# Projection units in groups of four, half of them opened by the lower rows, and fewer GpSimd splits in layer 1

## The chip, the cores and the metric

One core of a Trainium2 chip. The metric is the time of one execution of the whole kernel in microseconds of the device. Engines are named as in the profile: PE is TensorE (PEld its weight loads), DVE is VectorE, ACT is ScalarE, POOL is GpSimd, SP is SyncE, whose queue issues nearly all DMAs.

## The reference

Two layers, each attention and then a dense part, with the same weights in both layers. Everything is fp32; S = 2048 rows, D = 640, H = 32 heads of Dh = 20, F = 1536.

```python
def _A_ref(x, wqkv, wo):
    qkv = transpose((x @ wqkv).reshape(B, S, 3, H, Dh), 2, 0, 3, 1, 4)
    q, k, v = qkv[0], qkv[1], qkv[2]
    scores = einsum("bhqd,bhkd->bhqk", q, k) * (Dh ** -0.5)
    p = softmax(scores)
    o = einsum("bhqk,bhkd->bhqd", p, v)
    return transpose(o, 0, 2, 1, 3).reshape(B, S, D) @ wo

def _B_ref(x, w1, b1, w2, b2):
    h = relu(einsum("bsd,df->bsf", x, w1) + b1) ** 2
    return einsum("bsf,fd->bsd", h, w2) + b2

for _ in range(2):
    x = x + _A_ref(layernorm(x), wqkv, wo)
    x = x + _B_ref(layernorm(x), w1, b1, w2, b2)
```

## The kernel before

**Precision.** Every fp32 matrix is split into a high part in the matmul's own rounded format and a low part, the rest. A product of two matrices is three matmuls: high by high, high by low, low by high. A split is made in one of two ways: `split_to` (L253; ACT casts the high part out of the bank at L255, DVE subtracts at L256) or `split_on_pool` (L258; ACT copies the bank to SBUF at L262, POOL casts at L267 and subtracts at L270).

**Stages of a layer.** The projections (`qkv`, L674), attention (L932), then the output projection and the dense part. In attention each of 512 key tiles takes a score matmul (L556), an exponential on ACT (L563) and two matmuls with v (L568).

**The projections.** There are 72 units of work. 40 of them give a group of 128 columns of q or k for a block of 512 rows (`tb` is the block, `pos` the column group; the first sixteen are pos 0 to 3 of the blocks 0 to 3). 32 give half of the columns of v for 128 rows (`tt`, `hf`). A unit is 2 x 15 products into one PSUM bank. 15 contract over the upper 64 rows of the array and 15 over the lower 64 rows, and the two halves of the array can work at the same time on different units (`product`, L302; all products have line L320). Both halves add to the same bank. Where the upper 15 are done, a tiny copy on ACT (L322), the mark, is tied to the last of them, and the first lower product waits for the mark. The open units' banks are a ring of four (`ps_pj`).

`work_on` gives one stream of rows its next product; the upper stream and the lower stream both go through the units in order, and the lower one starts when the upper one is a unit and nine products (`LAG`) ahead. When the lower one ends a unit, `end` evicts it: q and k by `end_qk` (a split, three-fold stores to DRAM, L76 on SP; of the first k units also differences, kd), v by `end_v` (a copy on ACT, L368). Loads of q, k and kd from DRAM come back as operands of score matmuls.

**What is put between the products.** `front` (L376) prepares the normalised, transposed and split input of a block (x scaled at L251, transposes at L393 or, for block 0 of layer 1, L1259, splits of five pieces `xnT`), a step at a time. `insert` puts score matmuls (L474) for the row maxima of softmax between the products. Such a score takes either the upper or the lower half of the rows, and they come in pairs. A maximum is then taken by DVE (L486), or by ACT (L495) and DVE together (L503). A planner with estimated times of the engines (`now`, `busy`) chooses which score goes in and when; all this is settled while the program is built. What maxima are not placed in the projections are placed in attention, where cycles of eight key tiles take 12 or more pairs of them.

**The main loop** of the projections runs over j, 72 + 2 units, and offers each stream an insertion, else a product:

```python
while at_now[0] < (j + 1) * N and at_now[1] < len(chains) * N:
    if not insert(0):
        work_on(0)
    if not insert(1) and at_now[0] - at_now[1] > N + LAG + (not at_now[1]):
        work_on(1)
```

In layer 1 the weights of the first four column groups are cast and split first (`begin_first`, L1243): two of them ahead of the loop and two in it, one of the latter with DVE's subtraction. Blocks 2 and 3 are split by POOL in both layers (`tb > 1`), blocks 0 and 1 by ACT and DVE.

Of the kernel before, what the change touches and what calls it, by code (L numbers as in the profile page):

```python
# [8 lines left out]
F32 = mybir.dt.float32  # L9
# [7 lines left out]
P = 128  # L17
# [5 lines left out]
KD = D // P  # L23
NF = F // P
QB = 512
# [14 lines left out]
def tile_layers(  # L40
# [26 lines left out]
    def slot(shape, dtype, label):  # L67
        return arena.tile(shape, dtype, tag="slot", name=name(label))
# [225 lines left out]
    def after(later, earlier):  # L294
        tc.add_manual_dep(
            later.ins,
            earlier.ins.name,
            mybir.DependencyInfo(mybir.DependencyClass.Sync, mybir.DependencyReason.DATA),
            reason="lower rows add to the bank that the upper rows have left",
        )  # L300

    def product(ch, n, r):  # L302

        what, a, b = ch["of"]
        rows = slice(64 * r, 64 * r + 64)
        k, t = divmod(n, 3)
        if what == "qk":
            hw, hx = THREE[t]
            w = w_qk.piece(b * 10 + hw * KD + k)[rows]
            x = xt_[a][k][rows, hx, :]  # L310
            pair, width = (w, x), QB
        else:
            tb, i = divmod(a, 4)
            hx, hw = THREE[t]
            x = xt_[tb][k][rows, hx, i * P : (i + 1) * P]
            pair, width = (x, w_v.piece(k * 4 + hw * 2 + b)[rows]), HALF
        first, last = r == 0 and n == 0, r == 1 and n == 3 * KD - 1
        if first:
            ch["dst"] = ps_pj("pj")
        m = nc.tensor.matmul(ch["dst"][:, :width], *pair, start=first, stop=last)  # L320
        if n == 3 * KD - 1 and r == 0:
            mark = nc.scalar.copy(mark_t[:, 0:1], mark_t[:, 1:2])  # L322
            after(mark, m)
            ch["upper"] = mark
        if n == 0 and r == 1:
            after(m, ch.pop("upper"))

    def end_qk(pos, tb, dst):
        ev = slot([P, 2, QB], F32R, "ev")
        which, jj = divmod(ORDER[pos], 5)  # L330
        rows = slice(jj * P, (jj + 1) * P)
        kd = None
        if which and pos < FIRST:


            if tb % 2 == 0 and jj == 0:
                keys["of"] = slot([P, 2, QB], F32, "kf")
            kf = keys["of"][:, jj, :]
            r = xtile("r")[:, :QB] if tb % 2 else kf
            if tb:  # L340
                split_on_pool(ev[:, 0, :], ev[:, 1, :], dst, r)
            else:
                split_to(ev[:, 0, :], ev[:, 1, :], dst)
                nc.scalar.copy(r, dst)
            if tb % 2:
                kd = slot([P, 2, QB], F32R, "kd")
                nc.gpsimd.tensor_sub(kf, r, kf)
                pool_hi(kd[:, 0, :], kf)
                pool_lo(kd[:, 1, :], kf, kd[:, 0, :].bitcast(F32))
                if jj:  # L350
                    del keys["of"]
        else:
            (split_on_pool if tb or pos > 3 else split_to)(ev[:, 0, :], ev[:, 1, :], dst)

        def store():
            thrice(d_qk[which, tb, rows], ev, 1 + which)
            if kd is not None:
                thrice(d_kd[tb // 2, rows], kd, 2)

        return store  # L360
# [12 lines left out]
            v = vs.pop(tt)  # L373
            return lambda: dma(nc.sync, d_v[tt * P : (tt + 1) * P], v)

    def front(tb, x_src, bank, each=1):  # L376

        rows = [row_tile(x_src, tb * 4 + i) for i in range(4)]
        yield 0, False
        mvs = []  # L380
        for x in rows:
            mvs.append(stats(x))
            yield 1.1, False
        for n, (x, mv) in enumerate(zip(rows, mvs)):
            normalise(nc.vector, x, mv)
            yield 0.65, n == 3
        res = []
        for k0 in range(0, KD, each):
            ks = range(k0, min(k0 + each, KD))
            dsts = [bank("xt") for _ in ks]  # L390
            for k, dst in zip(ks, dsts):
                for i in range(4):
                    nc.tensor.transpose(  # L393
                        dst[:, i * P : (i + 1) * P], rows[i][:, k * P : (k + 1) * P], ident
                    )
            for dst in dsts:
                t = slot([P, 2, QB], F32R, "xnT")
                (split_on_pool if tb > 1 else split_to)(t[:, 0, :], t[:, 1, :], dst)
                res.append(t)
            if len(res) == KD:  # L400
                xt_[tb] = res
                rows.clear()
            yield 0, len(res) < KD
# [270 lines left out]
    def qkv(first, x_src, rest):  # L674
# [11 lines left out]
        def at(when, n, f):  # L686
            when.setdefault(n, []).append(f)

        for pos in range(2 if first else FIRST, 10):
            n = UNITS.index((0, pos)) - 4 if pos >= FIRST else pos - 2  # L690
            if first:
                if pos >= FIRST:
                    at(early, n - 2, lambda pos=pos: raws.append(raw_cols(wqkv, ORDER[pos])))
                at(late, n, lambda pos=pos: w_qk.put(
                    raws.pop(0), pos * 10, pos * 10 + KD, KD, nc.scalar.copy,
                    nc.vector.tensor_sub if pos == 2 else pool_lo,
                ))
            else:
                at(early, n, lambda pos=pos: w_qk.need(pos * 10, pos * 10 + 9))
# [55 lines left out]
        def later(keep=0):  # L755
            while len(pending) > keep:
                pending.pop(0)()
# [79 lines left out]
        N, LAG = 3 * KD, 9  # L837

        def end(n):

            what, a, b = chains[n]["of"]
            dst = chains[n].pop("dst")
            now["act"] = max(now["act"], now["pe"]) + 0.6
            if what == "qk":
                pending.append(end_qk(b, a, dst))
                if b >= FIRST and a == NQB - 1 or n == 4 * FIRST - 1:
                    w_qk.past(b * 10 + 9, w_qk.got)
                return
            f = end_v(a, b, dst)
            if not b:  # L850
                return
            later()
            pending.append(f)
            if a % 4 == 3:
                del xt_[a // 4]
            if a == 14:
                for c in (1, 3):
                    if (2, c) not in k_t:
                        load_k(2, c, True)
            if a == 10:  # L860
                load_v(0, 0)
            if a == 12:
                for c in range(4):
                    assert (0, c) not in k_t
                    load_k(0, c, True)
                load_q(1)

        at_now = [0, 0]

        def work_on(r):  # L870
            n, m = divmod(at_now[r], N)
            at_now[r] += 1
            if n < len(chains):
                product(chains[n], m, r)
                if r and m == N - 1:
                    end(n)

        for j in range(len(chains) + 2):
            if j < len(UNITS):
                while UNITS[j][0] not in xt_:  # L880
                    step_rest()
                run(early, j)
            while at_now[0] < (j + 1) * N and at_now[1] < len(chains) * N:
                if not insert(0):
                    work_on(0)
                if not insert(1) and at_now[0] - at_now[1] > N + LAG + (not at_now[1]):
                    work_on(1)
                now["pe"] += 0.235 if j < len(UNITS) else 0.155
                state["n"] += 1
                if state["n"] % 4 == 0 and not state["turn"]:  # L890
                    step_rest()
# [2 lines left out]
                w_v.save_full(1)  # L894
            if j < len(UNITS):
                run(late, j)
                later(1)
            n = j - 2
            if 1 < n < NQB * FIRST + 2:
                b, step = divmod(n - 2, 4)  # L900
# [425 lines left out]
```

## Time and profile before

| | us |
|---|---|
| median of 3 runs | 3692.89 (3692.02 to 3696.78) |
| the profiled execution's own time | 3689.96 |
| its span in the profile | 3688.1 |
| mean granted TensorE clock | 0.993 |
| projections of layer 1 | 0 to 357 |
| attention, output and dense part of layer 1 | 357 to 1860 |
| projections of layer 2 | 1883 to 2178, with a start from 1860 |
| attention, output and dense part of layer 2 | 2178 to 3690 |

The stage bounds are where the first score of attention (L556) and the first products of a layer stand in the trace. A row of the profile's windows has, for each engine, busy us and the count of its instructions. A row of the groups has line, engine, operation, output and inputs, count, then busy us and mean ns of one, then idle us just before and what ended it. A row of the chain has start, length and what it was.

### The profile page before, as it was taken

How to read it: one execution, taken by the hardware profiler on the slowest of the kernel's cores; microseconds unless marked ns; L12 is line 12 of the kernel's file. 1: busy time of each engine (PE TensorE's matmuls, PEld its weight loads, DVE VectorE, ACT ScalarE, POOL GpSimd, SP SyncE). 2: the span in 40 equal slices, each digit the busy share in tenths (PEclk: the TensorE clock that was granted, in tenths of full speed). 3: DMA queues.
4: the chain of work that ended last, by engine and by line, in shares of the span. 5: the costliest groups of instructions: out<-in, count | busy, mean ns of one | idle time of the engine just before them, and what ended most of it. 6: DMA issues, size and time to landing. Idle time of an engine off the chain costs nothing.

```text
span 3688.1 us, 67591 instructions
## 1 busy us (share of the span) xinstructions
PE 3635.3 (99%) x25738; PEld 2174.8 (59%) x25738; DVE 2714.6 (74%) x5034; ACT 2655.9 (72%) x5217; POOL 823.6 (22%) x914
## 2 busy tenths in 40 slices
PE   7899999999999999999999999999999999999999
PEld 5788433434334335988888873343433434378998
DVE  6677999999999993344567779999999999723443
ACT  2577999999999996122226789999999999941221
POOL 6440334321122111111144202112112211201110
PEclk8999999999999999999999999999999999999999
DMA  7776554432222135611167753232232121373111
GB/s 231 240 271 184 148 164 135 138 82 65 60 54 58 36 91 175 248 43 43 58 214 268 236 153 81 66 77 60 67 79 55 47 57 45 109 248 139 43 48 38
DMA packets 256880, 429.45 MB, mean 116 GB/s; under 512 B 60624, under 2 KB 107472, under 8 KB 256556
## 3 DMA queue, kind: packets, MB, share of 16 engines
q1 hardware_dynamic: 255724, 422.77, 37.3%
q8 instruction: 202, 3.31, 0.4%
q10 hardware_dynamic: 832, 2.37, 0.2%
q14 instruction: 122, 1.00, 0.1%
HBM read 265.15 MB, written 159.88 MB: 115 GB/s over the span
## 4 chain that ended last, share of the span: by engine, by line
PE 94%; DMA 2%; DVE 2%; ACT 1%; POOL 1%; issue 0%; SPq 0%; ACTq 0%; DVEq 0%
PE banks L568 28%; PE banks L285 20%; PE banks L556 20%; PE banks L474 15%; PE banks L320 9%; DMA q<-d_qk 1%; POOL xnT L270 1%; DVE h L256 0%; DMA d_qk<-ev 0%; PE banks L1112 0%; DVE r L1139 0%; ACT h L255 0%; DMA raw<-in_A_wqkv_dram 0%; DMA k<-d_qk 0%; ACT r L1138 0%; PE banks L393 0%
## 5 line engine op out<-in xcount | busy, mean ns | idle before, releaser
L563 ACT ACTIVATE e<-banks 128x512 f32<-128x512 f32 x4096 | 2113.3, 604 | 61.3 <-PE banks L474 2.2
L486 DVE TENSOR_REDUCE mx<-banks 128x1 f32<-128x512 f32 x3040 | 1908.8, 684 | 222.0 <-PE banks L474 146.8
L474 PE MATMUL banks<-k,q 60*128 60x512 f32 x3568 | 1243.4, 428 | 22.3 <-DMA q<-d_qk 20.6
L556 PE MATMUL banks<-q,k 62*128 62x512 f32 x4096 | 1153.0, 436 | 0.9 <-ACT rl L495 0.9
L568 PE MATMUL banks<-e,vg 128*32 128x512 f32 x8192 | 1094.1, 606 | 0.0
L556 PEld LDWEIGHTS banks<-q,k 62*128 62x128 f32 x4096 | 600.3, 185 | 702.5 <-ACT e L563 670.9
L474 PEld LDWEIGHTS banks<-k,q 60*128 60x128 f32 x3568 | 582.1, 185 | 300.0 <-DVE mx L486 206.5
L503 DVE CUSTOM_DVE_ANT_0 rl<-banks,rl 128x512 f32<-128x512 f32 x528 | 345.5, 689 | 106.4 <-PE banks L474 90.8
L320 PE MATMUL banks<-xnT,wqk 64*128 64x512 f32 x2400 | 393.0, 400 | 3.1 <-DVE xnT L256 3.1
L568 PEld LDWEIGHTS banks<-e,vg 128*32 128x32 f32 x8192 | 162.1, 108 | 358.0 <-issue 331.7
L285 PE MATMUL banks<-w,h 128*128 128x320 f32 x2304 | 358.5, 313 | 5.9 <-DVE h L256 3.8
L495 ACT ACTIVATE rl<-banks 128x512 f32<-128x512 f32 x534 | 288.2, 600 | 99.7 <-PE banks L474 94.6
L285 PEld LDWEIGHTS banks<-w,h 128*128 128x128 f32 x2304 | 340.6, 189 | 15.4 <-DVE h L256 8.2
L285 PE MATMUL banks<-xnT,w 128*128 128x512 f32 x1440 | 330.0, 390 | 0.0
L320 PEld LDWEIGHTS banks<-xnT,wqk 64*128 64x128 f32 x2400 | 301.8, 190 | 37.6 <-DVE xnT L256 3.5
L1138 ACT ACTIVATE r<-banks,b_t 128x512 f32<-128x512 f32 x96 | 66.1, 689 | 356.7 <-PE banks L285 352.8
L285 PEld LDWEIGHTS banks<-xnT,w 128*128 128x128 f32 x1440 | 269.6, 188 | 55.0
L267 POOL CAST mr<-nt 128x32 fp32r<-128x32 f32 x64 | 13.4, 209 | 1197.5 <-DVE nt L529 1197.5
L612 POOL TENSOR_TENSOR few<-few,minus_t 128x16 f32<-128x16 f32 x62 | 179.8, 2900 | 152.6 <-DMA few<-d_s 152.6
L320 PE MATMUL banks<-wv,xnT 64*128 64x320 f32 x1920 | 200.5, 307 | 0.4 <-DMA wv<-d_wv 0.4
L1158 DVE TENSOR_TENSOR x<-banks,x 128x320 f32<-128x320 f32 x128 | 62.9, 492 | 182.9 <-PE banks L285 181.2
L320 PEld LDWEIGHTS banks<-wv,xnT 64*128 64x128 f32 x1920 | 190.9, 186 | 2.1 <-DMA wv<-d_wv 0.8
(78 smaller groups left out, 1969.3 us busy)
## 6 DMA issues: line engine op xcount, KB each, us to landing
q<-d_qk SPq DMA_DIRECT2D x256, 240.0 KB
d_qk<-ev SPq DMA_DIRECT2D x80, 512.0 KB
k<-d_qk SPq DMA_DIRECT2D x156, 240.0 KB
x<-d_x SPq DMA_DIRECT2D x88, 320.0 KB
d_qk<-ev SPq DMA_DIRECT2D x80, 256.0 KB
d_o<-ot SPq DMA_DIRECT2D x248, 80.0 KB
ot<-d_o SPq DMA_DIRECT2D x38, 512.0 KB
d_v<-v SPq DMA_DIRECT2D x32, 512.0 KB
```

What stands on the lines that cost most here:

```text
L285: nc.tensor.matmul(dst, a, b, start=(n == 0), stop=(n == last))
L320: m = nc.tensor.matmul(ch["dst"][:, :width], *pair, start=first, stop=last)
L474: nc.tensor.matmul(dst, q_t[t][b : b + 60, p, sub * P : (sub + 1) * P], k_t[t // NQB, c][b : b + 60, p, :], start=True, stop=True,)
L486: nc.vector.tensor_reduce(maxima(t)[:, 2 * par + p, sub, c : c + 1], dst, axis=AX.X, op=ALU.max)
L495: nc.scalar.activation(res, dst, AF.Relu)
L503: nc.vector.tensor_tensor_reduce(out=r, in0=dst, in1=r, scale=1.0, scalar=LEAST, op0=ALU.add, op1=ALU.max, accum_out=maxima(t)[:, 2 * par ...
L556: nc.tensor.matmul(dst, k_t[t // NQB, kt // 4][b : b + 62, p, (kt % 4) * P : (kt % 4 + 1) * P], q_t[t][b : b + 62, p, :], start=True, stop ...
L563: nc.scalar.activation(es[p][:, par, :], dst, AF.Exp, scale=SCALE)
L568: nc.tensor.matmul(acc[32 * h : 32 * h + 32, :], v_t[t // NQB, kt // 8][:, kt % 8, 32 * h : 32 * h + 32], es[p][:, par, :], start=(kt == 0 ...
L612: nc.gpsimd.tensor_tensor(few, few, minus_t, op=ALU.pow)
L1138: nc.scalar.activation(r, dst, AF.Relu, bias=b1_t[:, f : f + 1])
L1158: nc.vector.tensor_add(x[:, c], dst[:, :HALF], x[:, c])
```

## The change

Units are worked in groups of four. In each group the upper stream goes through units 0, 1, 2, 3 and the lower stream through 2, 3, 0, 1. So each stream opens two units and closes two, both streams start together and end together, and `LAG` goes. The mark works both ways: it stands between the half that opens a unit and the half that closes it. Two units are ended in the third and two in the fourth quarter of a group.

Since both streams use a group's units from the start, the order of the weights is changed: pos 0 and 2 ahead of the loop, pos 1 and 3 before its first unit, all of them with POOL's subtraction. `keys` counts its four users rather than being opened and dropped by block, the stores follow the order in which units end, and v's loads move accordingly.

Which `xnT` pieces POOL splits is now said by the caller of `front`: in layer 1, k = 1 of block 2 and k = 1 and 3 of block 3 (all five of each before). In layer 2, all of block 2 as before, and k = 1 and 3 of block 3 (all five before). The others go to `split_to`.

```diff
-    def product(ch, n, r):
+    def product(ch, n, r, opens):
...
-        first, last = r == 0 and n == 0, r == 1 and n == 3 * KD - 1
+        first, last = opens and n == 0, not opens and n == 3 * KD - 1
...
-        if n == 3 * KD - 1 and r == 0:
+        if n == 3 * KD - 1 and opens:
             mark = nc.scalar.copy(mark_t[:, 0:1], mark_t[:, 1:2])
             after(mark, m)
-            ch["upper"] = mark
-        if n == 0 and r == 1:
-            after(m, ch.pop("upper"))
+            ch["half"] = mark
+        if n == 0 and not opens:
+            after(m, ch.pop("half"))
...
-            for dst in dsts:
+            for k, dst in zip(ks, dsts):
                 t = slot([P, 2, QB], F32R, "xnT")
-                (split_on_pool if tb > 1 else split_to)(t[:, 0, :], t[:, 1, :], dst)
+                (split_on_pool if k in on_pool else split_to)(t[:, 0, :], t[:, 1, :], dst)
...
+        if first:
+            for pos in (1, 3):
+                at(early, 0, lambda pos=pos: w_qk.put(
+                    raws.pop(0), pos * 10, pos * 10 + KD, KD, nc.scalar.copy, pool_lo
+                ))
...
-                    raws.pop(0), pos * 10, pos * 10 + KD, KD, nc.scalar.copy,
-                    nc.vector.tensor_sub if pos == 2 else pool_lo,
+                    raws.pop(0), pos * 10, pos * 10 + KD, KD, nc.scalar.copy, pool_lo
...
         def work_on(r):
-            n, m = divmod(at_now[r], N)
+            s, m = divmod(at_now[r], N)
+            if s == len(chains):
+                return
             at_now[r] += 1
-            if n < len(chains):
-                product(chains[n], m, r)
-                if r and m == N - 1:
-                    end(n)
+            n = s // 4 * 4 + (s + 2 * r) % 4
+            product(chains[n], m, r, s % 4 < 2)
+            if s % 4 > 1 and m == N - 1:
+                end(n)
...
-        for j in range(len(chains) + 2):
+        for j in range(len(chains)):
...
-            while at_now[0] < (j + 1) * N and at_now[1] < len(chains) * N:
-                if not insert(0):
-                    work_on(0)
-                if not insert(1) and at_now[0] - at_now[1] > N + LAG + (not at_now[1]):
-                    work_on(1)
+            while min(at_now) < (j + 1) * N if j + 1 == len(chains) else at_now[0] < (j + 1) * N:
+                for r in range(2):
+                    if not insert(r):
+                        work_on(r)
...
-                later(1)
+                later(sum(e // 4 * 4 + 2 + e % 2 == j for e in ended))
...
-        for n, _ in enumerate(front(2, d_x[1], ps_all)):
+        for n, _ in enumerate(front(2, d_x[1], ps_all, 1, range(KD))):
...
-        yield from front(3, d_x[1], ps_q, 2)
+        yield from front(3, d_x[1], ps_q, 2, (1, 3))
...
-        for pos in range(FIRST):
+        for pos in (0, 2, 1, 3):
             raws.append(raw_cols(wqkv, ORDER[pos]))
...
-        for pos in range(2):
+        for pos in (0, 2):
             w_qk.put(raws.pop(0), pos * 10, pos * 10 + KD, KD, nc.scalar.copy, pool_lo)
...
-        steps = [front(tb, x_in, ps_q, 2) for tb in (1, 2, 3)]
+        steps = [front(tb, x_in, ps_q, 2, (1, 3)[: tb - 1]) for tb in (1, 2, 3)]
```

More of the change, by code (lines that the diff above doesn't have):

```diff
@@ L298, in after @@
             mybir.DependencyInfo(mybir.DependencyClass.Sync, mybir.DependencyReason.DATA),
-            reason="lower rows add to the bank that the upper rows have left",
+            reason="one half of the rows adds to the bank that the other half has left",
         )
-    def product(ch, n, r):
+    def product(ch, n, r, opens):
         what, a, b = ch["of"]
@@ L333, in end_qk @@
         if which and pos < FIRST:
-            if tb % 2 == 0 and jj == 0:
-                keys["of"] = slot([P, 2, QB], F32, "kf")
+            if not keys:
+                keys.update(of=slot([P, 2, QB], F32, "kf"), left=4)
             kf = keys["of"][:, jj, :]
@@ L349, in end_qk @@
                 pool_lo(kd[:, 1, :], kf, kd[:, 0, :].bitcast(F32))
-                if jj:
-                    del keys["of"]
+            keys["left"] -= 1
+            if not keys["left"]:
+                keys.clear()
         else:
@@ L374, in end_v, with front @@
             return lambda: dma(nc.sync, d_v[tt * P : (tt + 1) * P], v)
-    def front(tb, x_src, bank, each=1):
+    def front(tb, x_src, bank, each=1, on_pool=()):
         rows = [row_tile(x_src, tb * 4 + i) for i in range(4)]
@@ L687, in at @@
             when.setdefault(n, []).append(f)
-        for pos in range(2 if first else FIRST, 10):
-            n = UNITS.index((0, pos)) - 4 if pos >= FIRST else pos - 2
+        if first:
[3 more added lines that the diff above has]
+                ))
+        for pos in range(FIRST, 10):
+            n = UNITS.index((0, pos)) - 4
             if first:
-                if pos >= FIRST:
-                    at(early, n - 2, lambda pos=pos: raws.append(raw_cols(wqkv, ORDER[pos])))
+                at(early, n - 2, lambda pos=pos: raws.append(raw_cols(wqkv, ORDER[pos])))
                 at(late, n, lambda pos=pos: w_qk.put(
-                    raws.pop(0), pos * 10, pos * 10 + KD, KD, nc.scalar.copy,
-                    nc.vector.tensor_sub if pos == 2 else pool_lo,
+                    raws.pop(0), pos * 10, pos * 10 + KD, KD, nc.scalar.copy, pool_lo
                 ))
@@ L836, in qkv @@
         chains += [{"of": ("v", tt, hf)} for tt in range(NKT) for hf in range(2)]
-        N, LAG = 3 * KD, 9
+        N, at_now, ended = 3 * KD, [0, 0], []
         def end(n):
@@ L843, in end, with work_on @@
             now["act"] = max(now["act"], now["pe"]) + 0.6
+            ended.append(n)
+            full = len(ended) % 4 == 0
             if what == "qk":
                 pending.append(end_qk(b, a, dst))
-                if b >= FIRST and a == NQB - 1 or n == 4 * FIRST - 1:
-                    w_qk.past(b * 10 + 9, w_qk.got)
+                if full and n >= 4 * FIRST - 4:
+                    w_qk.past(max(b, FIRST - 1) * 10 + 9, w_qk.got)
                 return
             f = end_v(a, b, dst)
-            if not b:
-                return
[L852 to L870, printed above, removed]
-            n, m = divmod(at_now[r], N)
-            at_now[r] += 1
-            if n < len(chains):
-                product(chains[n], m, r)
-                if r and m == N - 1:
-                    end(n)
-        for j in range(len(chains) + 2):
+            if b:
+                later(1)
+                pending.append(f)
+                if a == 10:
+                    load_v(0, 0)
+                if a == 12:
+                    for c in range(4):
+                        assert (0, c) not in k_t
+                        load_k(0, c, True)
+                    load_q(1)
+                if a == 14:
+                    for c in (1, 3):
+                        if (2, c) not in k_t:
+                            load_k(2, c, True)
+            if full and a % 4 > 1:
+                del xt_[a // 4]
+        def work_on(r):
+            s, m = divmod(at_now[r], N)
+            if s == len(chains):
+                return
+            at_now[r] += 1
+            n = s // 4 * 4 + (s + 2 * r) % 4
[3 more added lines that the diff above has]
+        for j in range(len(chains)):
             if j < len(UNITS):
```

## The prediction

> **What bounds the kernel now.** I read the page's first lines, then TensorE's list of waits over each layer's projections, then the windows, then the chain of work.
>
> ```profile
> PE 3635.3 (99%) x25738; PEld 2174.8 (59%) x25738; DVE 2714.6 (74%) x5034; ACT 2655.9 (72%) x5217; POOL 823.6 (22%) x914
> ...
> PE 94%; DMA 2%; DVE 2%; ACT 1%; POOL 1%; issue 0%; SPq 0%; ACTq 0%; DVEq 0%
> ```
>
> TensorE is busy nearly everywhere and the chain lies on it. So the time is the number of TensorE's slots times their length, plus the few places where it stands. The waits over the projections of layer 1 (0 to 360 us; three of the rows), then of layer 2 (1860 to 2180):
>
> ```profile
> PE banks L474 <- DMA q<-d_qk: 19.4, 4, 11.6
> PE banks L1259 <- POOL x L251: 10.3, 1, 10.3
> PE banks L393 <- DVE x L251: 5.0, 6, 2.4
> ```
>
> ```profile
> PE banks L474 <- DMA q<-d_qk: 1.5, 3, 0.8
> ```
>
> Layer 1 loses 19.4 us to loads of q; layer 2 hardly waits. Two more questions decide the change: what one product costs when the other half of the rows is idle, and how full the projection stages are otherwise. The windows of the products' line alone, then two windows of all engines:
>
> ```profile
> 18.00:27.00 9.00, 9.00 (x22) 6.97 (x23) 0.53 0.73 272
> 1877.00:1882.00 5.00, 4.97 (x22) 4.03 (x23) 1.00 0.87 277
> 1882.17:1885.10 2.93, 2.93 (x25) 2.41 (x24) 1.00 0.16 63
> ```
>
> ```profile
> 28.00:99.00 71.00, 53.65 (x389) 41.07 (x386) 40.65 (x77) 17.26 (x38) 43.12 (x55) 0.88 0.70 223
> 184.00:357.00 173.00, 172.87 (x1781) 160.13 (x1778) 130.59 (x399) 128.89 (x299) 49.08 (x62) 1.00 0.70 230
> 1883.00:2178.00 295.00, 290.48 (x2757) 253.66 (x2754) 223.40 (x626) 184.28 (x420) 100.21 (x121) 1.00 0.71 235
> ```
>
> The columns are stretch, length, busy us and count of TensorE, of its weight loads, and in the second fence of VectorE, ScalarE and GpSimd; then granted clock, share and GB/s of the DMAs. From 1877.00 the upper rows work alone: 22 products in 5.00 us, 0.227 each. From 1882.17 both halves work: 25 recorded products, 12.5 pairs, in 2.93 us, 0.234 a pair. So a lone product costs as much as a pair: a slot with one half idle is a slot lost. From 184 on TensorE is busy 172.87 of 173 us, so a slot saved there is saved in the end.
>
> **The idle half.** Today the lower rows start 24 products after the upper ones in each layer and end 24 after them. With units in groups of four both start and end together, and the stage takes 1080 slots of products where it took 1104. The 24 that go are worth qk slots, because today the last 24 lower qk products lie beside the shorter v products: 24 x 0.2275 = 5.46 us a layer, once in each, **-5.46 and -5.46**. In layer 1 the start is at half clock (0.53) and its early stage is held by loads, below; TensorE reaches each load as early as now, with 24 or 25 more products behind it, and these are taken back where it is full, after 184.
>
> By the Trainium skill ("TensorE: Matmul & The Clock Gate", What's actually happening) about 3.4 us of sustained work opens the clock; the row above, still at 0.53 over 18 to 27 us, disagrees while only half of the rows work. If the page held with both halves busy, layer 1's early products would take half as long; by the same rows that shortens only the way to the next load, so the sum has nothing for it.
>
> **The inserted maxima.** The planner inserts score products into the streams while the program is built, so the two orders of instructions can be counted. Fewer are placed in the projections: 587 become 554 in layer 1, and 603 become 569 in layer 2. Each takes one half of a slot: 33/2 x 0.2275 = **-3.75** and 34/2 x 0.2275 = **-3.87**. Attention takes them over: 1464 become 1496, and 1448 become 1484. What one costs there, from the chain: one block of attention with 48 maxima in 16 tiles, one with none.
>
> ```profile
> 2249.53 1.00 PE banks L568 x8
> ...
> 2281.40 0.99 PE banks L568 x8
> ```
>
> ```profile
> 3234.20 0.99 PE banks L568 x8
> ...
> 3258.66 1.00 PE banks L568 x8
> ```
>
> ```profile
> L563 ACT ACTIVATE e<-banks 128x512 f32<-128x512 f32 x65 | 33.7, 603 | 1.0
> L486 DVE TENSOR_REDUCE mx<-banks 128x1 f32<-128x512 f32 x48 | 30.1, 684 | 2.8 <-PE banks L474 1.7 <-PE banks L556 1.1
> ```
>
> Fifteen tiles take 31.87 us with maxima, 2.125 each; twelve take 24.46 without, 2.038. Three maxima a tile cost 0.087 us, 0.03 each: ScalarE sets the pace (33.7 of 34 us in the third fence, the groups of 2249 to 2283), not they. So 32 x 0.03 = **+0.96** and 36 x 0.03 = **+1.08**. But in 20 cycles of eight tiles there will be 13 pairs of maxima where there were 12, which the trace does not show. Two more maxima cost 0.06 us by this row, or 2 x 30.1/48 = 1.26 us if VectorE has no room. It has 2.8 us idle in 34, room for 4 more at 0.63 in 16 tiles, just what two such cycles need; hence I take the low end. The high end would be 20 x 1.2 = +24 us, and below nothing it cannot go, as each adds a matmul.
>
> **Layer 1's chain to the q loads.** This is the unsure term. The chain between 42 and 125 us:
>
> ```profile
> 45.23 0.62 POOL xnT L267
> 45.92 1.28 POOL xnT L270
> ...
> 58.97 3.87 DVE x L251 x3
> 62.89 0.49 PE banks L393
> ...
> 74.34 1.30 POOL ev L270
> ...
> 78.67 5.71 DMA d_qk<-ev
> 84.46 5.86 DMA k<-d_qk
> 90.33 8.65 DMA q<-d_qk
> 99.07 0.76 PE banks L474
> ...
> 114.45 6.57 DMA q<-d_qk
> ```
>
> And from the timeline of the same stretch, the first loads' waits and the second stall (in brackets the idle time before, and what ended it):
>
> ```profile
> 53.47 0.47 PE L474 MATMUL banks<-k,q 60*128 60x512 f32 x1 [0.33 <-DMA q<-d_qk]
> ...
> 54.42 0.73 PE L474 MATMUL banks<-k,q 60*128 60x512 f32 x3 [0.48 <-DMA q<-d_qk]
> ...
> 121.11 0.76 PE L474 MATMUL banks<-k,q 60*128 60x512 f32 x1 [6.92 <-DMA q<-d_qk]
> ```
>
> Four groups of layer 1, for the prices:
>
> ```profile
> L270 POOL TENSOR_TENSOR xnT<-r,xnT 128x512 fp32r<-128x512 f32 x10 | 12.9, 1285 | 0.8
> L256 DVE TENSOR_TENSOR xnT<-banks,xnT 128x512 fp32r<-128x512 f32 x10 | 6.3, 684 | 6.5 <-ACT xnT L255 6.5
> L251 DVE TENSOR_SCALAR x<-x,mv 128x640 f32<-128x640 f32 x15 | 11.4, 792 | 1.8 <-POOL mv L247 1.7
> L368 ACT COPY v<-banks 128x320 f32<-128x320 f32 x32 | 13.9, 433 | 9.9 <-PE banks L320 5.8 <-PE banks L474 2.6 <-issue 1.6
> ```
>
> GpSimd now splits all ten xnT pieces of blocks 2 and 3, 0.62 + 1.29 = 1.9 us each; three remain, so 7 x 1.9 = 13.3 us leave it. VectorE gets 7 x 0.68 = 4.8 us, and ScalarE casts in place of copies, at the same length. VectorE is busy 40.65 of 71 us there, so that is covered by its idle time; without the cover it would be +4.8. In layer 2 block 2 stays on GpSimd and three pieces of block 3 move, beside a stage where VectorE is busy 223.40 of 295 us: nothing.
>
> Freed GpSimd does not bring the loads forward by 13 us, since its order changes too. The transposes of block 3 stand 25 products later, at about 53.5 + 3 (the first load, below) + 5.5 = 62 us, against 62.89 now. Behind them GpSimd does two splits (3.8), then both K units of block 1, which close in one slot: each a cast, two subtractions, a cast and a subtraction, 2 x 0.62 + 3 x 1.29 = 5.1 us; then the first Q, 1.9. From 62.9 that is 62.9 + 3.8 + 10.2 + 1.9 = 78.8 us, where today the first Q of block 1 ends at 75.64. So 13.3 us less work is eaten by the second K that now stands ahead of that Q, and the loads that wait for it would land some 3 us later than 99.07, with 5.5 us more products done. The second stall (until 121.11) follows stores and loads on SP's queue that move the same way. The first wait for q, now under 1 us at 53.5 to 54.5, grows as well: the stores of one more K and one more Q unit, 1.5 MB, stand ahead of that load on SP; at 223 GB/s that is 6.7 us if none is hidden, 0 if all is; I take 3. These lost microseconds come out of stalls that TensorE already has: whoever comes later to 99 waits less. I take **0** for all stalls together; the bounds are -18.5 (both stalls gone, 11.6 + 6.9) and +6.7.
>
> Three normalisations on VectorE took 3.87 us at 58.97, 1.29 each, while GpSimd worked; the mean is 0.79. The Trainium skill ("SBUF — State Buffer", two separate sides) says that the two share a port pair under an exclusive lock and the loser waits for the whole instruction; the row agrees. By that rule, less GpSimd work would free a further 3 x 0.5 = 1.5 us of that chain, within the bounds.
>
> **Layer 2's first load** waits for stores in the same way; the rows of its chain:
>
> ```profile
> 1896.29 3.46 DMA d_qk<-ev
> 1900.24 3.90 DMA q<-d_qk
> 1904.17 0.73 PE banks L474 x3
> ```
>
> With both streams filled TensorE comes there no later, and the load stands behind one more store. One store takes 3.46 us, so 0 to 3.5; I take **+1.5**.
>
> **The banks** cost nothing if the forecast is right. Four banks hold the open units. Today a closed unit's bank is next opened 1.4 slots later; then one slot later, with two units closing at once. The line of v's evictions over layer 2's v units:
>
> ```profile
> 2080.00:2177.00 97.00, 13.41 (x31) 1.00 0.57 179
> ```
>
> 31 in 97 us: a v unit's slot lasts 3.1 us. Two evictions of 0.43 behind two activations of 0.6 (as in attention's group above) make 2.1 us, and leave 1.0. Handing a unit to the other rows has a whole slot where it had nine products.
>
> **Sum.** Layer 1: -5.46 - 3.75 + 0.96 + 0 = -8.25. Layer 2: -5.46 - 3.87 + 1.08 + 1.5 = -6.75. Together -15.0 on the profiled execution's 3689.96: 3675.0. The median of the runs shown stands 2.93 above that execution, so the forecast is **3678** us, with an own range of 3665 to 3685.
>
> **Rivals.**
> *The bank turn (slower, 0.14).* If ScalarE comes over 1.0 us later to a pair of evictions than reckoned, each opening slot stalls. There are 18 groups with two opening slots in two layers, 72; at 0.5 us each, 36 us: 3714. For it: two evictions fall together, and marks too. Against it: ScalarE is busy only 184.28 of 295 us in layer 2's stage. The Trainium skill ("TensorEngine Tiling (Array Packing)", PSUM Bottleneck) warns that tiling speeds TensorE and not the emptying of its banks.
> *The gain is eaten (within 0.2%, 0.12).* Loads land 6.7 us late in layer 1, and the 13-pair cycles cost 0.4 us each, 8 us: -15 + 6.7 + 8, about 3690 to 3692.
> *Both stalls of layer 1 vanish (faster, 0.08).* If SP issues the stores as soon as GpSimd is free, the 18.5 us go as well: 3678 - 18.5 = 3659.5.
> That the change does not do what it says is excluded by the counted order.
>
> **Chances.** The forecast has 0.66. A measurement of this kernel can tell about 0.2%, 7.4 us, from no change. Faster by more than that: 0.66 + 0.08 = 0.74; within it 0.12; slower by more 0.14. The range goes from the third rival to the second with some margin: 3659 to 3694; what lies outside is mostly the first rival.
>
> **What would show it.** In the profile after: no stretch of 5 us of lone products at 1877; products of layer 1 ended by about 8 us sooner with the waits on q still near 20 us; layer 2's stage some 8 us shorter; attention 1 us longer in each layer. Waits of the products' line on ScalarE's evictions would show the first rival; a wait list with no q load over 5 us the third. A VectorE above 97% in 13-pair cycles with ScalarE idle would prove the price of 0.03 wrong.

## The result and the profile after

The changed kernel takes 3722.0 us, median of 4 runs (3718.82 to 3723.6), against 3692.91 before; the ratio is 1.0076, with a 95% interval of 1.0058 to 1.0093. The forecast was 3678, faster, with a range of 3659 to 3694. The kernel is slower by some 29 us, and lies outside the range.

The profiled execution took 3718.82 us with a span of 3717.0. Its first part, then the waits of TensorE over the projections of layer 1 (0 to 360), some rows, and of layer 2 (1860 to 2180):

```profile
PE 3640.9 (98%) x25739; PEld 2183.2 (59%) x25739; DVE 2732.9 (74%) x5044; ACT 2645.6 (71%) x5183; POOL 805.3 (22%) x896
```

```profile
PE banks L475 <- DMA q<-d_qk: 25.9, 4, 14.6
PE banks L1263 <- POOL x L251: 10.3, 1, 10.3
...
PE banks L394 <- DVE x L251: 1.6, 2, 1.4
PE banks L320 <- ACT kf L344: 1.5, 1, 1.5
```

```profile
PE banks L475 <- DMA q<-d_qk: 12.7, 3, 8.8
...
PE banks L320 <- ACT kf L344: 0.4, 1, 0.4
```

(L474, L393, L1259, L556, L563, L568 and L486 of before are L475, L394, L1263, L557, L564, L569 and L487 here.) Cut at the first product, the first score of attention and the last copy of attention's sums of each layer, the two traces say where the time went:

| stage, us | before | after | difference | forecast |
|---|---|---|---|---|
| projections, layer 1 | 339.5 | 332.5 | -7.0 | -9.2 |
| attention, layer 1 | 1091.0 | 1110.2 | +19.2 | +1.0 |
| dense part, start of layer 2 | 428.6 | 428.9 | +0.3 | 0 |
| projections, layer 2 | 301.0 | 304.2 | +3.2 | -7.8 |
| attention, layer 2 | 1087.4 | 1099.7 | +12.4 | +1.1 |
| dense part | 422.7 | 423.4 | +0.7 | 0 |

Two things went wrong, then: attention, off by 29.5 us, and the projections of layer 2, off by 11. That the idle half is gone is plain. The products' line from layer 2's first product shows 26 in 3.00 us, pairs from the start, where before had 22 in 5.00:

```profile
1889.75:1892.75 3.00, 3.00 (x26) 2.50 (x28) 1.00 0.84 238
```

In attention, the groups of 472 to 508 us, which hold a cycle of 13 pairs and the cycle ahead of it (columns as in the prediction's groups):

```profile
L564 ACT ACTIVATE e<-banks 128x512 f32<-128x512 f32 x65 | 33.6, 604 | 2.8 <-PE banks L557 1.7 <-PE banks L475 0.6
L487 DVE TENSOR_REDUCE mx<-banks 128x1 f32<-128x512 f32 x52 | 32.6, 684 | 3.5 <-PE banks L475 2.3 <-PE banks L557 1.1
...
L475 PEld LDWEIGHTS banks<-k,q 60*128 60x128 f32 x50 | 7.8, 184 | 6.8 <-DVE mx L487 5.9
```

The last of these rows before, in the groups of 2249 to 2283:

```profile
L474 PEld LDWEIGHTS banks<-k,q 60*128 60x128 f32 x49 | 7.8, 185 | 4.2 <-DVE mx L486 3.4
```

ScalarE, which had 1.0 us idle in 34 before, has 2.8 in 36, ended mostly by TensorE's scores; and TensorE's weight loads for the maxima wait 5.9 us for the reductions, where they waited 3.4. The exponentials no longer set the pace alone. A cycle of eight key tiles has 32 exponentials, four a tile. Cut at every 32 of them, twenty cycles hold the scores of 26 maxima on TensorE and last 17.87 us on average, and the cycle ahead of each lasts some 17.7; the others last 17.0.

### The profile page after: what moved, and what is told of

Read it like the earlier page. It is cut to its first block, busy times and chain, and to the rows that moved or that the text cites. A ratio compares the mean times of both kernels' runs of the same rounds, so it can differ in the third digit from the quotient of the medians.

```text
span 3717.0 us, 67535 instructions
## 1 busy us (share of the span) xinstructions
PE 3640.9 (98%) x25739; PEld 2183.2 (59%) x25739; DVE 2732.9 (74%) x5044; ACT 2645.6 (71%) x5183; POOL 805.3 (22%) x896
## 4 chain that ended last, share of the span: by engine, by line
PE 93%; DVE 2%; DMA 2%; ACT 1%; POOL 1%; issue 0%; SPq 0%; ACTq 0%; DVEq 0%; POOLq 0%
PE banks L569 27%; PE banks L285 20%; PE banks L557 20%; PE banks L475 15%; PE banks L320 10%; DMA q<-d_qk 1%; DVE h L256 1%; DVE mx L487 1%; PE banks L1116 0%; DVE r L1143 0%; ACT h L255 0%; PE banks L394 0%; ACT r L1142 0%; DMA d_qk<-ev 0%; POOL ev L270 0%
## 5 line engine op out<-in xcount | busy, mean ns | idle before, releaser
L564 ACT ACTIVATE e<-banks 128x512 f32<-128x512 f32 x4096 | 2111.7, 604 | 95.0 <-PE banks L557 24.3
L487 DVE TENSOR_REDUCE mx<-banks 128x1 f32<-128x512 f32 x3108 | 1951.3, 684 | 250.9 <-PE banks L475 174.3
L475 PE MATMUL banks<-k,q 60*128 60x512 f32 x3603 | 1246.4, 431 | 44.3 <-DMA q<-d_qk 38.7
L557 PE MATMUL banks<-q,k 62*128 62x512 f32 x4096 | 1148.8, 434 | 1.5 <-DVE mx L504 0.9
L569 PE MATMUL banks<-e,vg 128*32 128x512 f32 x8192 | 1092.8, 605 | 0.0
L557 PEld LDWEIGHTS banks<-q,k 62*128 62x128 f32 x4096 | 599.9, 185 | 673.4 <-ACT e L564 643.1
L475 PEld LDWEIGHTS banks<-k,q 60*128 60x128 f32 x3603 | 583.8, 185 | 362.0 <-DVE mx L487 246.3
L504 DVE CUSTOM_DVE_ANT_0 rl<-banks,rl 128x512 f32<-128x512 f32 x495 | 320.5, 688 | 112.6 <-PE banks L475 97.0
L320 PE MATMUL banks<-xnT,wqk 64*128 64x512 f32 x2400 | 376.2, 403 | 5.3 <-DVE xnT L256 3.3
L569 PEld LDWEIGHTS banks<-e,vg 128*32 128x32 f32 x8192 | 161.5, 108 | 353.8 <-issue 332.6
L496 ACT ACTIVATE rl<-banks 128x512 f32<-128x512 f32 x500 | 269.2, 606 | 108.4 <-PE banks L475 103.9
L255 ACT CAST xnT<-banks 128x512 fp32r<-128x512 f32 x70 | 40.0, 587 | 211.8 <-PE banks L1116 129.9
L320 PE MATMUL banks<-wv,xnT 64*128 64x320 f32 x1920 | 188.6, 306 | 0.0
```

The lines of the kernel that those rows point to most:

```text
L475: nc.tensor.matmul(dst, q_t[t][b : b + 60, p, sub * P : (sub + 1) * P], k_t[t // NQB, c][b : b + 60, p, :], start=True, stop=True,)
L487: nc.vector.tensor_reduce(maxima(t)[:, 2 * par + p, sub, c : c + 1], dst, axis=AX.X, op=ALU.max)
L496: nc.scalar.activation(res, dst, AF.Relu)
L504: nc.vector.tensor_tensor_reduce(out=r, in0=dst, in1=r, scale=1.0, scalar=LEAST, op0=ALU.add, op1=ALU.max, accum_out=maxima(t)[:, 2 * par ...
L557: nc.tensor.matmul(dst, k_t[t // NQB, kt // 4][b : b + 62, p, (kt % 4) * P : (kt % 4 + 1) * P], q_t[t][b : b + 62, p, :], start=True, stop ...
L564: nc.scalar.activation(es[p][:, par, :], dst, AF.Exp, scale=SCALE)
```

## Experiments

**The 13-pair cycles alone, in the kernel before (before13).**

```diff
             n = min(max(round(state["debt"]), 12), 16)
+            if state["cycle"] in (THIRTEENS_1 if first else THIRTEENS_2):
+                n = 13
+            state["cycle"] += 1
```

(the two names stand for the 13 and the 7 cycles' numbers).

> The kernel before, with 13 pairs of maxima instead of 12 forced in the same 20 cycles of attention in which the changed kernel has them (13 in layer 1, 7 in layer 2); nothing of the projections changes, and the maxima end some cycles earlier. Theory (a 13-pair cycle costs about 1.45 us with the cycle ahead of it, whatever else the change does): attention of layer 1 grows from 1091.0 by about 13 x 1.45 - 0.7 = 18 us, of layer 2 from 1087.4 by about 10 us, the whole to about 3718. Rival (attention slows because of what the change leaves behind, later loads or splits): attention stays within 2 us and the whole near 3690.

3717.95 us, against 3688.01 of the kernel before on that chip. Attention took 1108.3 and 1098.8 us. The projections, 337.4 and 302.4, have the code of before, which took 339.5 and 301.0, so a difference of 2 us between single runs of a stage says nothing. VectorE's reductions (L486) over the two cycles of one such event and over the next, in windows cut at the exponentials:

```profile
547.53:565.21 17.68, 15.69 (x25) 1.00 0.52 172
565.21:583.29 18.08, 15.68 (x25) 1.00 0.23 58
583.29:600.31 17.02, 15.09 (x24) 1.00 0.58 188
```

This event costs 0.7 + 1.1 us over two cycles of 17.0, here with the reductions of its two extra maxima on both sides of the cut; the average is 1.56. The theory holds: these cycles alone cost the kernel before 17.3 + 11.4 = 28.7 us of attention, nearly all of the 31.6 that the change lost there.

**Another order of the 13-pair cycle (smooth13).**

```diff
-        13: "baanmbVmbanambbnbmVanbmnaVnaabnmbVanbmaanVnmbbanaVmnbmabVabbmmnaVm",
+        13: "naambbmVanmbambnVbmannabVnabnmabVabnmbanVbbmnanamVbmmbaanVbmbmnaaV",
```

> The changed kernel with another hand-written order for its 13-pair cycles: the 12-pair order with one lower maximum added to the second tile and one upper maximum to the sixth, so that no tile has more than four maxima (the order now in use has a tile with five). Theory A (the order of the 13-pair cycle, an uneven one, starves ScalarE): an event of 13 pairs falls from 1.45 us to 0.3 or less, attention to about 1095 and 1089 us, the whole to about 3692. Theory B (VectorE has no room for two more maxima in 17 us, whatever their order): an event keeps 1.0 us or more, the whole stays above 3708.

3720.07 us; attention 1108.4 and 1100.4. The reductions (L487) of a cycle with 26 maxima, and of one with 24:

```profile
387.87:406.30 18.43, 16.25 (x26) 1.00 0.48 133
423.42:440.40 16.98, 15.03 (x24) 1.00 0.39 94
```

The neighbour is spared, the cycle itself takes 18.43, and the event still costs 1.43. The order in which the maxima stand in the cycle is not the cause; their number is. Theory A falls. All engines over the same cycle (columns as in the prediction, VectorE's third):

```profile
387.87:406.30 18.43, 17.95 (x124) 7.11 (x124) 17.11 (x29) 16.53 (x32) 5.71 (x6) 1.00 0.48 133
```

VectorE is busy 93% of it, so it is not simply full, as theory B puts it.

**A cycle's price against its number of maxima (cycle11).**

```diff
+        11: "naambbVanmbambVbmannabVnabnmabVabnmbanVbbmanaVbmmbaanVbmbmnaaV",
...
+            if first and 6 <= state["cycle"] < 18:
+                n = 11
+            if first and 30 <= state["cycle"] < 42:
+                n = 13
```

> The kernel before, with 11 pairs of maxima in twelve cycles of layer 1's attention (the 12-pair order with one maximum of each half taken out) and the pairs made up later in cycles of 13 to 16; the total of maxima is the same. It prices a cycle against its number of maxima. Theory (a cycle takes the longer of ScalarE's 16.3 us and 0.708 us a maximum, 17.0 / 24 = 18.43 / 26): 11 pairs take 16.3 us, 13 take 18.4 or 17.9 + 0.7 by the neighbour, 16 take 22.7. Rival (0.03 us a maximum below 24, as the prediction had it): 11 pairs take 16.9.

The whole took 3712.11 us, attention of layer 1 1111.1. Cycles with 22, 24, 26, 32 and no maxima; the windows of all engines (columns as in the prediction, VectorE's third):

```profile
478.12:494.86 16.74, 16.74 (x120) 6.94 (x120) 13.88 (x22) 16.32 (x32) 5.91 (x7) 1.00 0.78 246
778.29:795.30 17.01, 17.01 (x122) 6.80 (x122) 15.92 (x27) 16.53 (x32) 3.33 (x3) 1.00 0.39 92
951.65:969.69 18.04, 18.04 (x124) 7.35 (x123) 16.84 (x29) 16.53 (x33) 3.37 (x3) 1.00 0.30 71
703.02:724.52 21.50, 20.68 (x136) 7.72 (x128) 20.42 (x36) 16.74 (x34) 3.33 (x3) 1.00 0.30 101
1402.12:1418.42 16.30, 16.30 (x98) 5.41 (x96) 1.72 (x4) 16.11 (x32) 3.37 (x3) 1.00 0.28 77
```

On average the twelve cycles of 22 took 16.69 us, those of 24 17.0, a run of thirteen cycles of 26 17.95, two of 32 21.3. So the price of a maximum is (16.69 - 16.30)/22 = 0.018 us up to 22, 0.155 from 22 to 24, 0.47 from 24 to 26 and 0.56 from there to 32, where VectorE is busy 20.42 of 21.50 us and ScalarE only 16.74. The 0.47 holds for 13-pair cycles in a row; one alone between cycles of 12, as the change has them, cost 1.4 to 1.6 us, 0.7 to 0.8 a maximum, and why it costs more was not separated. Both expectations missed: 11 pairs take neither 16.3 nor 16.9, and 16 pairs 21.3 rather than 22.7. The curve bends where ScalarE's 16.3 us and VectorE's reductions come together, and the kernel before stands right at the bend: 1464 maxima in attention are 732 pairs, what 61 cycles of 12 hold.

**More maxima in the projections, none too many in attention (fill).**

```diff
-                now["pe"] += 0.235 if j < len(UNITS) else 0.155
+                now["pe"] += 0.235 if j < len(UNITS) else 0.17
```

> The changed kernel with one number of the planner changed: a slot of the v units counts 0.17 us instead of 0.155, so that 32 more maxima go into the projections of each layer (586 and 601) and attention has exactly the 1464 and 1448 of the kernel before, without a 13-pair cycle. Theory (attention is slower by the 13-pair cycles alone, since 732 pairs are all that 61 cycles of 12 hold): attention back to 1091 and 1087.5 us; the projections grow by 16 slots of 0.147, 2.4 us a layer, the whole to about 3691. Rival (attention is slower for other reasons): attention stays 10 us or more above the kernel before.

3702.03 us. Attention took 1088.8 and 1088.9 us, as before the change; the cause of its 31.6 us is closed. But the projections took 340.2 and 310.8 us, 7.7 and 6.6 more than in the changed kernel, where 2.4 were expected: 0.22 us a maximum instead of 0.07. The waits on q moved less (28.1 and 13.2 us, from 25.9 and 12.7), so this is mostly the price of the scores themselves.

**One K and one Q close together (order).**

```diff
-    UNITS = [(tb, pos) for tb in range(NQB) for pos in range(FIRST)]
+    UNITS = [(tb, pos) for tb in range(NQB) for pos in (0, 2, 1, 3)]
```

with the weights put in the matching order.

The chain of the changed kernel that led there, at its 8.85 us stall in layer 2:

```profile
1928.47 0.61 POOL ev L267
...
1937.69 1.29 POOL kd L270
...
1941.54 1.27 POOL ev L270
1942.82 0.37 SPq L76
...
1945.52 4.84 DMA q<-d_qk
1950.36 0.14 issue
1950.50 0.76 PE banks L475
```

> The changed kernel with the first sixteen units in the order K, K, Q, Q in place of K, Q, K, Q within a block, so that one K and one Q unit close in a slot rather than both K and then both Q; the weights are put in the matching order. The 13-pair cycles stay. Theory (the stalls on loads of q come from GpSimd doing both K units, 5.1 us each, ahead of the first Q): the 8.85 us stall in layer 2 falls to under 3, the first loads land about 4 us sooner in both layers, the 14.6 us stall of layer 1 shrinks by 5 or more; the whole falls by 10 to 20 us to about 3700. Rival (the loads are held by the DMA queues): the waits on q stay within 3 us of 25.9 and 12.7.

3721.01 us; the waits on q are 27.8 and 14.0 us, the stall is 8.84 us. The theory falls, and the rival's number came. SP's queue and TensorE in the run's timeline, at the stall:

```profile
1940.72 2.74 SPq L76 DMA_DIRECT2D d_qk<-ev  x4
1945.90 0.80 SPq L76 DMA_DIRECT2D d_kd<-kd  x2
1946.80 1.44 SPq L76 DMA_DIRECT2D k<-d_qk  x2
1948.28 0.94 SPq L76 DMA_DIRECT2D q<-d_qk  x2
...
1953.57 0.76 PE L475 MATMUL banks<-k,q 60*128 60x512 f32 x1 [8.84 <-DMA q<-d_qk]
```

The first Q's split ended at 1935.5 here, 43.4 us after layer 2's first product instead of 51.2, and won nothing: the loads of k and q stand on SP behind the stores of all four units, of which the last is now a kd at 1945.90. My theory named the wrong queue. In layer 1 the first Q of block 1 was split by 72.2 us instead of 81.3, and the large stall ended at 100.3 instead of 101.2.

**The same, with the loads issued ahead of the second stores (early).**

```diff
+            if j < NQB * FIRST and j % 4 == 3 and PLAIN[j // 4][0]:
+                tiles(PLAIN[j // 4][0][0])
             n = j - 2
```

> The kernel of the run named order (units K, K, Q, Q, one K and one Q close together), and the first loads of k and q of each block are issued one unit sooner: on SP's queue they stand ahead of the stores of the second K and Q, not behind them. The 13-pair cycles stay. Theory (SP's queue works in order, and the loads wait there behind stores and kd stores that wait for GpSimd's last piece): the 8.8 us stall of layer 2 falls by 7 or more, the 14.3 us stall of layer 1 by 7 to 10, the first waits (about 4 us in each layer) by 2 or more; the whole falls by 15 to 25 us against the 3721 of the run named order, to about 3700. Rival (the loads' own transfer or TensorE's earlier arrival sets the stalls): the two large stalls stay within 2 us.

3706.06 us, 15 less. The same place in the timeline:

```profile
1930.61 1.37 SPq L76 DMA_DIRECT2D k<-d_qk  x2
1932.03 0.92 SPq L76 DMA_DIRECT2D q<-d_qk  x2
1933.00 3.25 SPq L76 DMA_DIRECT2D d_qk<-ev  x4
1936.76 1.18 SPq L76 DMA_DIRECT2D d_kd<-kd  x2
1937.86 0.47 PE L475 MATMUL banks<-k,q 60*128 60x512 f32 x1 [2.27 <-DMA q<-d_qk]
```

and the waits in layer 1, then layer 2:

```profile
PE banks L475 <- DMA q<-d_qk: 20.2, 2, 11.7
```

```profile
PE banks L475 <- DMA q<-d_qk: 6.3, 4, 2.9
```

The loads now stand ahead of the stores, and the 8.8 us stall is 2.3. Layer 2's projections take 295.7 us, 5.3 less than before the change, and layer 1's 329.0, 10.5 less. That is what the whole change brings there when SP's order fits it, with the 33 and 34 maxima fewer that attention then pays for. Layer 1's largest stall gave up less than expected: 11.7 us from 14.3.

**Only the groups, and only the splits (groups_only, splits_only).**

```diff
 groups_only, in the changed kernel:
-        steps = [front(tb, x_in, ps_q, 2, (1, 3)[: tb - 1]) for tb in (1, 2, 3)]
+        steps = [front(tb, x_in, ps_q, 2, range(KD) if tb > 1 else ()) for tb in (1, 2, 3)]
 splits_only, in the kernel before:
-        steps = [front(tb, x_in, ps_q, 2) for tb in (1, 2, 3)]
+        steps = [front(tb, x_in, ps_q, 2, (1, 3)[: tb - 1]) for tb in (1, 2, 3)]
```

(and the like for block 3 of layer 2; splits_only also has `front`'s new parameter).

> The changed kernel with GpSimd still splitting all ten xnT pieces of blocks 2 and 3 in layer 1 and all five of block 3 in layer 2: the groups of four alone. Theory (the moved splits take 13 us of GpSimd's work off the chain to the q loads): layer 1's stalls on q grow by 5 to 13 us, so the projections of layer 1 go from 332 to about 340 us, layer 2 stays within 1 us. Rival (the moved splits do nothing that matters, as SP's queue sets the loads): layer 1's projections stay within 2 us of 332.

> The kernel before with only the moved splits (three xnT pieces on GpSimd in layer 1 rather than ten, three fewer in block 3 of layer 2), units and streams as before, so attention is the same. Theory: the 11.6 us stall on q in layer 1 shrinks by 5 to 11 us, the rest is unchanged, the whole about 3680. Rival (SP's queue or the DMAs set that stall): within 2 us of the kernel before.

3730.24 and 3689.51 us. The waits of layer 1 on q, groups first, then splits:

```profile
PE banks L475 <- DMA q<-d_qk: 32.3, 4, 20.1
```

```profile
PE banks L474 <- DMA q<-d_qk: 18.8, 4, 11.7
```

With the groups the moved splits are worth 338.5 - 332.5 = 6.0 us of layer 1: the largest stall is 20.1 us without and 14.6 with them. In the kernel before they take nothing off the 11.6 us stall, and 1.7 us off the stage, which is within the 2 us that runs differ by; the expectation of some 3680 missed. One run each; the two numbers in layer 2 (305.7 and 302.8) move by under 2 us.

**Both remedies together (early_fill, early_qk247, early_qk255).** `early` with the planner's slot lengths changed: 0.17 for v; or 0.247 or 0.255 for qk.

> The kernel of the run named early (order K, K, Q, Q and loads ahead of the second stores on SP) together with the planner's 0.17 us a v slot of the run named fill: 586 and 601 maxima in the projections, no 13-pair cycle. If the two effects add: projections 329.0 + 7.7 = 336.7 and 295.7 + 6.6 = 302.3 us, attention 1089 in each layer, the whole about 3688, the same as before within 0.2%.

> The same, but the planner's slot of the qk units counts 0.247 us instead of 0.235 and that of v stays 0.155: 585 and 597 maxima, no 13-pair cycle; the added maxima go into qk slots, where a pair of scores costs one slot of 0.2275 us, and not into v slots of 0.147. Theory (the 0.22 us a maximum of the run named fill comes from scores that lengthen the shorter v slots): 31 and 28 more maxima cost 15 slots, 3.5 us a layer, not 7; projections about 332.5 and 299 us, the whole about 3681. Rival (VectorE and ScalarE set that price in either place): projections near 336 and 302, the whole near 3688.

> The same with 0.255 us a qk slot: 610 and 610 maxima in the projections, attention of 1440 each. Theory: 25 and 13 more maxima than with 0.247 cost 0.11 us each in the projections, and attention wins 0.7 us for each cycle without maxima, one or two a layer: within 3 us of the run named early_qk247. Rival (the engines beside TensorE are full by then, and it waits for banks): 5 us or more slower than that.

| | median us | ratio to before | projections 1, 2 | attention 1, 2 |
|---|---|---|---|---|
| early_fill | 3686.2 | 0.9986 (0.9977 to 0.9996) | 334.8, 304.2 | 1089.3, 1087.5 |
| early_qk247 | 3678.6 | 0.9967 (0.9956 to 0.9978) | 322.0, 306.3 | 1088.9, 1089.7 |
| early_qk255 | 3687.0 | 0.9991 (0.9982 to 1.0001) | 330.1, 310.4 | 1088.6, 1087.8 |

early_qk247 beats both kernels, by 12 us and some 43 us. Its reason is not the one expected. Layer 2's projections cost 306.3 - 295.7 = 10.6 us for 28 more maxima, more than the rival had; layer 1 won because its waits on q fell:

```profile
PE banks L475 <- DMA q<-d_qk: 5.4, 1, 5.4
```

from 20.2 in early, so that the stage is 7.0 us shorter with 31 more maxima. Other maxima now lie between the products and the loads, but which of the shifted places did it was not separated.

## Why the prediction was wrong

- **Attention: the price of the maxima.** This step failed. The prediction put 0.03 us on a maximum, a mean between cycles with none and cycles with 24, and took the low end, 0.06 us, for a 13-pair cycle because VectorE had 2.8 us idle in 34. The runs show 1.4 to 1.6 us an event, 20 events, +31.6 us; even the high end I kept, 1.26 us, was too low. A mean price over a range with a bend in it says nothing at its upper end. The size of a reduction was not the error: with the 684 ns of its own row in place of 0.63 us, four more take 2.7 us and would still have fitted into the 2.8. Nor did VectorE have to be full: the sign that the prediction set for this, VectorE above 97%, never came (93% in smooth13's cycle). I priced two more maxima as if idle time anywhere in a block could be used. My reading is that TensorE, between banks that reductions have to free (5.9 us of waits) and scores that ScalarE waits for (2.3 us), could not use it; the runs show the number of maxima as the cause, not this path.
- **The 13-pair cycles themselves** were counted rightly, from the order of instructions: 732 to 748 pairs and 724 to 742.
- **The idle half.** -5.46 us a layer stands up, but only once the stalls are taken apart. The run early_fill has nearly the maxima of before in layer 2's projections (601 against 603). TensorE's row over that stage (length, busy us and count, clock, DMAs) before, in the changed kernel and in early_fill, the latter two with their stretches at half clock below:

```profile
1877.00:2178.00 301.00, 296.48 (x2784) 1.00 0.71 235
```

```profile
1889.70:2193.90 304.20, 289.24 (x2751) 0.98 0.71 229
1919.32:1926.15 6.83, 6.43 (x27) 0.50 0.61 144
1946.62:1953.44 6.82, 2.94 (x14) 0.50 0.97 244
```

```profile
1869.20:2173.40 304.20, 294.31 (x2783) 0.99 0.70 231
1898.55:1902.00 3.45, 3.45 (x16) 0.51 0.64 254
1932.70:1936.10 3.40, 3.24 (x15) 0.50 1.02 245
```

  A product took 0.41 us at a clock of 0.53 and 0.227 at 1.00, so as an estimate half of the busy time at half clock is lost: 4.7 us in the changed kernel and 3.3 in early_fill. TensorE's work at full clock is then 296.5 us before, 291.0 in early_fill and 284.6 in the changed kernel. At nearly equal maxima it falls by 5.5 us, as forecast. In the changed kernel it falls by 11.9, TensorE stands 10.4 us more, and 4.7 go to the half clock: +3.2, as measured. So the stalls cost more than their own length, and the prediction had no term for that.
- **Fewer maxima in the projections.** The -3.87 was too small by the same estimate: the 32 that the changed kernel has fewer than early_fill account for 291.0 - 284.6 = 6.4 us, 0.20 each instead of 0.114. Adding them back costs 0.22 us each in fill, and 0.38 in layer 2 of early_qk247, where the waits on q stay (6.4 us against 6.3).
- **Layer 2's loads.** This step failed too. The first wait was forecast at +1.5 and came to 3.9 us, from 1.3. The second, 8.85 us, was not seen, because the prediction left layer 2 out as a layer that "hardly waits", though it had the same units and the same queue in view for layer 1. The queue that holds the loads is SP's, shown by order and early: GpSimd's pieces count as far as a store waits for them at the head of that queue.
- **Layer 1's loads.** "0 for all stalls together" was 6.5 us too good for q (25.9 from 19.4), beside 3.4 us less waiting for normalised x. The first load came to 56.3 us, 3.85 us late; the forecast of 3 was a guess between 0 and 6.7. The first large stall ended at 101.2 (forecast some 102), but that was luck in part: the forecast took the end of the first Q's split as what the loads wait for (78.8 us; it came at 81.3), and in order that split ended 9 us sooner and the stall only 0.9. The moved splits paid 6.0 us there, and were needed.
- **The bank turn**, the rival on the slower side, had the right sign and not the cause: waits of products on evictions are 1.5 and 0.4 us in all.

## What to carry to other kernels

Before moving work from one stage to another, price it in the stage that receives it at that stage's margin: force one more of it into the kernel as it is, since a mean over a range tells nothing where two engines come level. A store that waits for its data at the head of SP's queue held every later load here, so when units are made to end together, look at what then stands between their stores and the next loads. Count a stall of TensorE with the half clock that comes with it. Groups of four gained only with both mended.

## What the runs showed of the hardware

The clock opened with both halves at work. Over the products of layer 1's start, 18 to 27 us, the kernel before had 22 products and a clock of 0.53; the changed one:

```profile
18.00:27.00 9.00, 8.85 (x64) 7.67 (x64) 0.81 0.93 304
```

64 products, at a mean clock of 0.81. If that is a half clock and then a full one, it opened 9.0 x 0.19/0.5 = 3.4 us after 18 us, which is an estimate from this row. It agrees with the window of about 3.4 us that the Trainium skill gives ("TensorE: Matmul & The Clock Gate", What's actually happening). Before, the upper rows worked alone over these 9 us, 0.41 us a product, and the clock did not open. After them both halves worked, and the clock was at half for some microseconds more:

```profile
27.50:31.40 3.90, 3.90 (x17) 2.61 (x14) 0.50 0.01 2
31.40:35.00 3.60, 1.36 (x7) 0.48 (x6) 0.90 0.38 150
```

17 products in 3.90 us are 0.23 each, pairs at half clock. By the same working on the last row it opened 3.6 x 0.10/0.5 = 0.7 us after 31.4, 14 us after the first product and some 5 after the lower rows had joined. So one half of the rows alone did not open the clock here in 9 us; a clock that was open stayed so over 5 us of it (1.00 from 1877.00). The gain in time was small: TensorE came to the first load of q at 52.5 us, 53.1 before, and then waited 3.85 us for it.
